# A price on changes of the matrix array's mode in a kernel's static order, with another order of its first loads

## The chip, the cores and the metric

The kernel runs on one core of one Trainium2 chip. The metric is the device time of one execution in microseconds (us); a lower one is better. Several runs are taken, and their median is given. A profile of one execution says what each engine did and when.

## What is computed

The reference runs a gated linear attention, a dense feed-forward layer and a layer of four experts, one after the other, all in float32.

```python
for t in range(S):                      # B, H, S, D = 2, 8, 768, 40
    m_new = np.maximum(f_gate[:, :, t] + m, i_gate[:, :, t])
    f_stab = np.exp(f_gate[:, :, t] + m - m_new)
    i_stab = np.exp(i_gate[:, :, t] - m_new)
    C = f_stab * C + i_stab * np.einsum('bhd,bhe->bhde', vt, kt)
    n = f_stab * n + i_stab * kt
    y[:, :, t] = o * (C @ qt) / np.maximum(np.abs(n @ qt), 1.0)
x = y as 1536 tokens x 320
h = x @ w_in                            # 320 x 2048
x = (h * (1.0 / (1.0 + np.exp(-1.702 * h)))) @ w_out
for e in range(4):                      # 320 x 1024, 1024 x 320
    out += p[:, e:e + 1] * (np.maximum(x @ w1[e], 0.0) @ w2[e])
```

## The kernel before, in words

**Attention.** The 768 steps are cut into 12 units of 64, and a unit holds both batches, 128 rows. A unit is worked in chunked form by `attn`: the decay of each pair of steps comes from two small matmuls with gate rows (`pe`, L343, and `pdc`, L347) and exponentials on ScalarE (`ex`, L353, and `dc`, L362); the scores `ps` (L380) are multiplied with `ex` to `pp` (L388); `pv` (L439, L442) is scores times values plus queries times the state; `sd` (L415) is what the unit adds to the state `st` (L424, L426), and `vw`, `ds` and `qs` (L397, L404, L368) scale values, state and queries, on VectorE or GpSimd. Then come the division and the output gate (L453 to L468), a transpose through TensorE (`pt`, L484), and its copy into the tiles `xb` in a high and a low half (L492, L496). `ps`, `sd` and `pv` run on 64 x 64 pieces of the array, two at a time; all other matmuls of the first 250 us use the whole 128 x 128 array. Most of the attention's PSUM tiles come from a pool of three (`at`).

**Dense layer.** The 2048 hidden features are 16 chunks. A chunk's weights come as 64-bit numbers (`raw`, L508, 704 KB) and are turned into a high and a low float32 half in seven operations by `conv` (L512 to L541) on ScalarE, VectorE and GpSimd. `layer1` (L574) and the second product (L663 to L668, called y here) run for three blocks of 512 tokens; the first block's chunks 0 to 3 are done in two halves of 256 tokens, since its later units are not there yet. Between the two products stand a tanh, a product, and a split into halves (`moe1`).

**Experts.** From about 262 us on all is in place and TensorE works through the four experts (L588, L592, L760 to L762).

**The order.** Nothing is scheduled at run time. Attention, conversion and dense layer are given to a planner, `Plan`, each piece with an engine, an estimated length, a due time (from the tables `DUE`, `T0`, `R256`, `R512`, `LOAD` and `RAW0`), what it depends on and which buffers it takes and gives. `Plan.order` walks through a modelled time: it takes the engine that can start first, and of that engine's pieces that can start then the one with the earliest due time. The code is emitted in that order, and the chip's engines then run their own instructions strictly in it. All loads are issued on SyncE's queue in planned order as well (`ring`), and eight of them may be under way. Strings such as `VW` or `GL` name the engine of each piece that VectorE (D) or GpSimd (P) can do. Until the first layer-1 step, gaps in TensorE's plan are filled with warm-up matmuls (`wps`, L791); later ones are left out.

Of the kernel before, what the change touches and what calls it, by code (L numbers as in the profile page):

```python
# [44 lines left out]
NR = 4  # L45
LANES = 8
XI = (0, 1, 3, 4, 2)
RAW0 = -39.51
LOAD = (-39.53, 5.33)
T0 = 7.75  # L50
R512 = 2.72
R256 = 3.14
DUE = (0.97, 2.56, -5.05, -4.98, 16.69, 15.23, 40.06, 43.14, 47.58, 64.09, 67.93, 31.23)
VW = "DPDPDDDDPPDD"
DS = "PDPPPDPDPDDP"
QS = "DPDDDDPPDPDP"
ADD = "DDPDPPPDDDDDPPDP"
LO = "PPPPDDDPPPDDDDDD"
HI = "AAAPAAAAAAAAPAAA"
GL = "PPQDDPPPQDQQPPDQDQPDDQPDQPPDPQQDQDPPQPDDPDDPDPQQPPDP"  # L60
# [3 lines left out]
class Plan:  # L64
# [9 lines left out]
    def add(self, eng, dur, due, fn=None, deps=(), take=(), give=(), lag=0.1, shared=False):  # L74
        self.ops.append((eng, dur, due, fn, {d for d in deps if d is not None}, take, give, lag, shared))
        return len(self.ops) - 1

    def order(self, slack):
        ops = self.ops
# [8 lines left out]
        port = 0.0  # L88
        while ready:
            cand = []  # L90
            for k, r in ready.items():
                eng, dur, due, _, _, take, _, _, shared = ops[k]
                if any(not self.tokens[t] for t in take):
                    continue
                t0 = max([r, free.get(eng, 0.0) if eng else 0.0] + [min(self.tokens[t]) for t in take])
                if shared:
                    t0 = max(t0, port)
                cand.append((t0, due, k))
# [3 lines left out]
            eng = ops[first[2]][0]  # L102
# [4 lines left out]
            eng, dur, _, _, _, take, give, lag, shared = ops[k]  # L107
# [5 lines left out]
            if shared:  # L113
                port = end
# [26 lines left out]
def body(tc, qk, kv, og, gates, gblk, wa, wb, dp, cst, out):  # L141
# [3 lines left out]
    with outer:  # L145
# [32 lines left out]
        PE, DV, AC, PO, SP = "PE", "DVE", "ACT", "POOL", "SP"  # L178
# [144 lines left out]
        def attn(u, due):  # L323
            ld = loads[u]
# [57 lines left out]
            m = P.add(PE, 1.2, due - 6, mm_s, deps=[ld["qk"]], take=[tok])  # L382
# [10 lines left out]
            if not last:  # L393
# [23 lines left out]
                sd = P.add(PE, 1.2, due - 3.6, mm_sd, deps=[vw, ld["kv"]], take=["at"], give=["vw"])  # L417
# [26 lines left out]
            pv = P.add(PE, 2.1 if u else 1.2, due - 4, mm_pv, deps=[pp, qs, ld["kv"], state.get(u)], take=["at"], give=["pp"] + (["qs"] if u else []))  # L444
# [59 lines left out]
        def conv(c, due):  # L504
# [38 lines left out]
            ld = ring(RAW0 + 2.5 * c if c < NR else due - 12, 2.25, load, take=["raw"] if c >= NR else [], deps=[] if c == 0 else [gate[4]] if c == 1 else gate[1][1] if c == 2 else reads)  # L543
# [395 lines left out]
```

## Time and profile before

| what | us |
|---|---|
| median of 3 runs (608.62 to 609.77) | 609.72 |
| profiled execution, its own time | 609.17 |
| span of the profile | 607.2 |
| TensorE busy, matmuls | 597.9 (98%) |
| VectorE busy | 254.6 (42%) |
| ScalarE busy | 185.1 (30%) |
| GpSimd busy | 153.9 (25%) |

The span is shorter than the execution's own time by 2.0 us, which lie around it. Busy shares are means over very different stages: attention and conversion are over by 160 us. PE is TensorE, ACT is ScalarE, DVE is VectorE, POOL is GpSimd and SP is SyncE. The starts of matmuls are recorded and their ends modelled, so the time that a group of them takes is best read from its start to the start of what follows. Some matmuls show as two passes, so 16 of the attention's appear as 32.

### The profile page before, as it was taken

The page shows a single profiled execution, that of the slowest core. Times are in us where ns is not written, and L with a number is a line of the kernel's source. Part 1 is how long each engine was busy: PE and PEld are TensorE (multiplying, and loading weights), DVE is VectorE, ACT ScalarE, POOL GpSimd, SP SyncE. Part 2 cuts the span into 40 slices and gives each one's busy share as a digit, 9 for nine tenths or more (in the row PEclk, how much of TensorE's full clock was granted, in tenths as well). Part 3 has the DMA queues.
Part 4 walks back from the last instruction along what each step waited for, and adds up shares of the span by engine and source line. Part 5 has one row for each costly group of instructions (what it writes and reads, how often), then busy time and mean ns, then how long its engine had stood idle before and what let it go on. Part 6 is the DMA issues. An engine that isn't in the chain of part 4 may idle for free.

```text
span 607.2 us, 10194 instructions
## 1 busy us (share of the span) xinstructions
PE 597.9 (98%) x4356; PEld 510.7 (84%) x4360; DVE 254.6 (42%) x457; ACT 185.1 (30%) x310; POOL 153.9 (25%) x126
## 2 busy tenths in 40 slices
PE   7999999999999999999999999999999999999997
PEld 3689888888888888889888888888888888888886
DVE  5699888887333422353231323232323131322313
ACT  4557466544333523341111111111111111111111
POOL 0473265521010331298504710006600000000000
PEclk8999999999999999999999999999999999999999
DMA  8876446610000010034301310002200000001101
GB/s 230 236 244 200 130 160 191 186 40 1 2 0 2 1 47 1 0 96 135 103 1 44 101 49 1 1 1 83 61 1 0 1 1 0 1 4 41 44 1 43
DMA packets 14432, 37.69 MB, mean 62 GB/s; under 512 B 2132, under 2 KB 4660, under 8 KB 14388
## 3 DMA queue, kind: packets, MB, share of 16 engines
q1 hardware_dynamic: 14066, 36.83, 20.1%
q8 instruction: 34, 0.56, 0.4%
q10 hardware_dynamic: 322, 0.21, 0.2%
q14 instruction: 10, 0.08, 0.1%
HBM read 34.75 MB, written 2.16 MB: 61 GB/s over the span
## 4 chain that ended last, share of the span: by engine, by line
PE 89%; DVE 4%; DMA 3%; ACT 1%; issue 1%; SPq 1%; POOL 0%; DVEq 0%; ACTq 0%
PE l L592 24%; PE l L574 16%; PE acc L762 9%; PE acc L761 9%; PE acc L760 9%; DMA raw<-in_wa_dram 3%; PE l L588 2%; PE yA L663 2%; PE yA L665 2%; PE yA L664 2%; PE yB L663 2%; PE yC L667 2%; PE yB L665 2%; PE yC L668 2%; PE yB L664 2%; PE pv L439 1%
## 5 line engine op out<-in xcount | busy, mean ns | idle before, releaser
L592 PE MATMUL l<-xb,w 128*128 128x512 f32 x616 | 146.2, 394 | 0.0
L592 PEld LDWEIGHTS l<-xb,w 128*128 128x128 f32 x616 | 113.9, 188 | 31.0 <-issue 8.0
L744 DVE SCALAR_TENSOR_TENSOR gl<-l,gh 128x512 fp32r<-128x512 f32 x88 | 60.9, 692 | 183.6 <-ACT gh L743 183.6
L743 ACT ACTIVATE gh<-l 128x512 fp32r<-128x512 f32 x88 | 52.7, 598 | 259.6 <-PE l L592 259.6
L762 PE MATMUL acc<-w,gl 128*128 128x320 f32 x384 | 118.7, 309 | 0.0
L761 PE MATMUL acc<-w,gh 128*128 128x320 f32 x384 | 118.6, 309 | 0.0
L760 PE MATMUL acc<-w,gh 128*128 128x320 f32 x384 | 118.5, 309 | 0.0
L574 PE MATMUL l<-xb,w 128*128 128x512 f32 (+1 forms) x480 | 111.8, 378 | 0.6 <-DVE xb L496 0.6
L574 PEld LDWEIGHTS l<-xb,w 128*128 128x128 f32 x480 | 85.7, 188 | 17.2 <-DVE xb L496 0.9
L760 PEld LDWEIGHTS acc<-w,gh 128*128 128x128 f32 x384 | 72.1, 188 | 1.1
L761 PEld LDWEIGHTS acc<-w,gh 128*128 128x128 f32 x384 | 72.1, 188 | 1.1
L762 PEld LDWEIGHTS acc<-w,gl 128*128 128x128 f32 x384 | 72.1, 188 | 0.0
L561 POOL TENSOR_TENSOR w<-rawf,w 128x704 fp32r<-128x704 f32 x32 | 55.4, 1732 | 2.7
L560 POOL TENSOR_SCALAR w<-rawf 128x704 fp32r<-128x704 f32 x32 | 24.9, 780 | 105.8 <-PE acc L762 96.8
L648 POOL TENSOR_TENSOR gl<-g,gh 128x512 fp32r<-128x512 f32 (+1 forms) x21 | 24.5, 1165 | 107.4 <-ACT gh L643 104.8
L631 ACT ACTIVATE g<-l 128x512 f32<-128x512 f32 (+1 forms) x52 | 29.3, 564 | 63.3 <-PE l L574 62.4
L635 DVE SCALAR_TENSOR_TENSOR g<-g,l 128x512 f32<-128x512 f32 (+1 forms) x38 | 24.1, 635 | 40.9 <-ACT g L631 40.7
L769 DVE SCALAR_TENSOR_TENSOR osb<-acc,pd,osb 128x320 f32<-128x320 f32 x36 | 17.3, 545 | 39.5 <-PE acc L762 39.5
L643 ACT ACTIVATE gh<-g 128x512 fp32r<-128x512 f32 (+1 forms) x38 | 22.5, 592 | 22.8 <-DVE g L635 22.8
L439 PE MATMUL pv<-kvt,pp 64*64 64x41 f32 x384 | 22.5, 228 | 0.0
L791 PE MATMUL wps<-wt 128*128 128x512 bf16 x73 | 20.4, 431 | 1.8 <-DVE wt L787 1.2
L439 PEld LDWEIGHTS pv<-kvt,pp 64*64 64x64 f32 x384 | 19.7, 133 | 2.4 <-issue 1.4
(113 smaller groups left out, 702.3 us busy)
## 6 DMA issues: line engine op xcount, KB each, us to landing
raw<-in_wa_dram SPq DMA_DIRECT2D x16, 704.0 KB
rawf<-in_wb_dram SPq DMA_DIRECT2D x32, 352.0 KB
qkt<-in_qk_dram SPq DMA_DIRECT2D x12, 416.0 KB
kvt<-in_kv_dram SPq DMA_DIRECT2D x12, 324.0 KB
ot<-in_og_dram SPq DMA_DIRECT2D x6, 320.0 KB
out_dram<-osb SPq DMA_DIRECT2D x12, 160.0 KB
const<-in_cst_dram SPq DMA_DIRECT2D x1, 228.0 KB
lsc<-hl SPq DMA_DIRECT2D x1, 192.0 KB
```

The lines of the kernel that those rows point to most:

```text
L439: te.matmul(out=half(pv, b)[:, h, :], lhsT=half(tiles["pp", u], b)[:, h, :], rhs=half(x, b)[:, h, D:KV], start=True, stop=u == 0)
L560: po.tensor_scalar(out=w[:, 0:WC], in0=raw, scalar1=1.0, scalar2=0.0, op0=ALU.mult, op1=ALU.add)
L561: po.tensor_tensor(out=w[:, WC:2 * WC], in0=raw, in1=w[:, 0:WC].bitcast(F32), op=ALU.subtract)
L574: te.matmul(out=ps[:, 0:n], lhsT=w[:, k0:k0 + 128], rhs=x[xi], start=(i == 0), stop=(i == 7))
L592: te.matmul(out=ps, lhsT=W[c][:, k0:k0 + 128], rhs=x[xi], start=False, stop=(i == 6))
L631: sc.activation(out=g[:, 0:nn], in_=tiles["l1", n][:, 0:nn], func=AF.Tanh, scale=0.851)
L648: eng.tensor_tensor(out=gl[:, 0:nn], in0=g[:, 0:nn], in1=gh[:, 0:nn].bitcast(F32), op=ALU.subtract)
L743: sc.activation(out=gh, in_=ps, func=AF.Relu)
L744: ve.scalar_tensor_tensor(out=gl, in0=ps, scalar=0.0, in1=gh.bitcast(F32), op0=ALU.max, op1=ALU.subtract)
L760: te.matmul(out=ps, lhsT=a, rhs=w[:, 384:WC], start=st, stop=False)
L761: te.matmul(out=ps, lhsT=a, rhs=w[:, WC + 384:2 * WC], start=False, stop=False)
L762: te.matmul(out=ps, lhsT=b, rhs=w[:, 384:WC], start=False, stop=sp)
```

## The change

Each piece of the planner's work gets a mark `half`, set for the scores, the state's sum and `pv`, which use 64 x 64 pieces of the array. Where TensorE's pieces compete, one that would change the mode has 8.59 us added to its due time, and 0.15 us to its length when taken. The second weight chunk's load (`c == 1`) now depends on the second unit's loads having been issued, where both hung on a copy of the gates (`gx`, L231) before. And the numbers of the tables and the strings are set anew. Nothing is computed otherwise. In line numbers, the new kernel is four lines longer from L128 on.

```diff
+MODE = 8.59
-RAW0 = -39.51
-LOAD = (-39.53, 5.33)
-T0 = 7.75
+RAW0 = -58.95
+LOAD = (-38.58, 16.7)
+T0 = 0.44
...
-DUE = (0.97, 2.56, -5.05, -4.98, 16.69, 15.23, 40.06, 43.14, 47.58, 64.09, 67.93, 31.23)
-VW = "DPDPDDDDPPDD"
+DUE = (0.16, 1.74, -5.43, -4.9, 16.37, 15.12, 32.37, 41.15, 48.48, 68.35, 78.86, 41.0)
+VW = "DPDPDPPDPPDP"
...
     def order(self, slack):
...
-        port = 0.0
+        port, mode = 0.0, False
...
-                cand.append((t0, due, k))
+                cand.append((t0, due + (MODE if eng == "PE" and half != mode else 0), k))
...
-            eng, dur, _, _, _, take, give, lag, shared = ops[k]
+            eng, dur, _, _, _, take, give, lag, shared, half = ops[k]
+            if eng == "PE":
+                dur += 0.15 if half != mode else 0
+                mode = half
...
-            m = P.add(PE, 1.2, due - 6, mm_s, deps=[ld["qk"]], take=[tok])
+            m = P.add(PE, 1.2, due - 6, mm_s, deps=[ld["qk"]], take=[tok], half=True)
...
-            ld = ring(RAW0 + 2.5 * c if c < NR else due - 12, 2.25, load, take=["raw"] if c >= NR else [], deps=[] if c == 0 else [gate[4]] if c == 1 else gate[1][1] if c == 2 else reads)
+            ld = ring(RAW0 + 2.5 * c if c < NR else due - 12, 2.25, load, take=["raw"] if c >= NR else [], deps=[] if c == 0 else [loads[1]["qk"] - 1, loads[1]["kv"] - 1] if c == 1 else gate[1][1] if c == 2 else reads)
```

The marks on `sd` and `pv` are set in the same way. Over the whole program the strings move these pieces from VectorE to GpSimd: one of 11 query scalings (L368), two of 11 value scalings (L397), one of 16 chunk additions (L528) and three of 52 low halves of the dense layer (L648); and one high half of a chunk from ScalarE to GpSimd (L533 for L535).

The first place is the load queue of SyncE at the start of the program (`raw_102` to `raw_104` are the first three weight chunks, `gs` and `gx` belong to the gates). Before:

```order
L284 DMA qkt<-in_qk_dram 104x1024
L508 DMA raw_102<-in_wa_dram 128x1408
L289 DMA kvt<-in_kv_dram 128x648
L181 DMA gx<-gs_99 96x1x128
L508 DMA raw_103<-in_wa_dram 128x1408
L284 DMA qkt<-in_qk_dram 104x1024
L289 DMA kvt<-in_kv_dram 128x648
L181 DMA lt<-hl 8x2x64 x2
L181 DMA rr<-hl 2x8x128
L181 DMA lsc<-hl 96x4x128
L303 DMA ot<-in_og_dram 128x640
L508 DMA raw_104<-in_wa_dram 128x1408
```

And now:

```order
L512 DMA raw_102<-in_wa_dram 128x1408
L288 DMA qkt<-in_qk_dram 104x1024
L293 DMA kvt<-in_kv_dram 128x648
L185 DMA gx<-gs_99 96x1x128
L288 DMA qkt<-in_qk_dram 104x1024
L293 DMA kvt<-in_kv_dram 128x648
L512 DMA raw_103<-in_wa_dram 128x1408
L185 DMA lt<-hl 8x2x64 x2
L185 DMA rr<-hl 2x8x128
L185 DMA lsc<-hl 96x4x128
L512 DMA raw_104<-in_wa_dram 128x1408
L307 DMA ot<-in_og_dram 128x640
```

The first chunk stands ahead of the first unit's queries, the second unit's loads ahead of the second chunk, and the third chunk ahead of the first output gates (`ot`).

The second place is TensorE at the first two layer-1 steps (`l`), where the third and fourth units come in. Before:

```order
L791 MATMUL wps<-wt 128x512
L574 MATMUL l_474<-xb_73,w 128x256 x8
L380 MATMUL ps<-qkt 64x64 x16
L343 MATMUL pe<-rr,lt 128x512 x2
L574 MATMUL l_517<-xb_73,w 128x256 x8
L347 MATMUL pdc<-rr,ltd 128x512 x2
L380 MATMUL ps<-qkt 64x64 x16
L415 MATMUL sd<-vw,kvt 64x41
L415 MATMUL sd<-vw,kvt 40x41
```

And now:

```order
L795 MATMUL wps<-wt 128x512
L578 MATMUL l_470<-xb_73,w 128x256 x8
L347 MATMUL pe<-rr,lt 128x512
L351 MATMUL pdc<-rr,ltd 128x512
L347 MATMUL pe<-rr,lt 128x512
L578 MATMUL l_491<-xb_73,w 128x256 x8
L351 MATMUL pdc<-rr,ltd 128x512
L384 MATMUL ps<-qkt 64x64 x32
L419 MATMUL sd<-vw,kvt 64x41
L419 MATMUL sd<-vw,kvt 40x41
```

The third unit's scores stood between the two steps and the fourth's behind; now both stand behind the second step, in one piece with `sd`, and the small decay matmuls are spread ahead of them.

The third place is ScalarE from the first unit's copy into `xb` to the third unit's exponential (`raw_104` and `raw_105` are the third and fourth chunk, `ot` the tanh of output gates). Before:

```order
L492 ACTIVATE xb_73<-pt 128x3x128
L535 ACTIVATE w<-cx 128x704
L516 ACTIVATE cr<-raw_104 128x704
L512 ACTIVATE cx<-raw_105 128x704
L516 ACTIVATE cr<-raw_105 128x704
L492 ACTIVATE xb_73<-pt 128x3x128
L309 ACTIVATE ot<-ot 128x640
L535 ACTIVATE w<-cx 128x704
L631 ACTIVATE g<-l_474 128x256
L353 ACTIVATE ex<-pe 128x512 x2
```

And now:

```order
L496 ACTIVATE xb_73<-pt 128x3x128
L539 ACTIVATE w<-cx 128x704
L496 ACTIVATE xb_73<-pt 128x3x128
L313 ACTIVATE ot<-ot 128x640
L516 ACTIVATE cx<-raw_105 128x704
L520 ACTIVATE cr<-raw_105 128x704
L357 ACTIVATE ex<-pe 128x512
L366 ACTIVATE dc<-pdc 104x512
L357 ACTIVATE ex<-pe 128x512
L366 ACTIVATE dc<-pdc 104x512
```

Both conversions of the fourth chunk now stand between the tanh and the exponentials `ex` and `dc`; before, they stood ahead of the second unit's copy.

## Rows read from the trace of the kernel before

**Rows 1.** Busy time by stage: us, then each engine's busy (instructions), PEclk, DMA share, GB/s.

```profile
30.00:130.00 100.00, 98.52 (x1400) 84.23 (x1399) 89.28 (x171) 61.48 (x104) 47.86 (x37) 1.00 0.57 175
...
160.00:600.00 440.00, 440.00 (x2343) 383.15 (x2342) 127.10 (x198) 96.80 (x162) 95.53 (x76) 1.00 0.10 28
```

**Rows 2.** TensorE in order of time, first 45 us: start, length, line, operands, idle before.

```profile
7.77 1.44 PE L380 MATMUL ps<-qkt 40*64 40x64 f32 x32 [2.13 <-DMA qkt<-in_qk_dram]
...
18.35 1.15 PE L380 MATMUL ps<-qkt 40*64 40x64 f32 x32
...
32.22 0.47 PE L574 MATMUL l<-xb,w 128*128 128x256 f32 x1
...
33.28 1.09 PE L574 MATMUL l<-xb,w 128*128 128x256 f32 x7 [0.60 <-DVE xb L496]
...
37.85 1.15 PE L380 MATMUL ps<-qkt 40*64 40x64 f32 x32 [0.28 <-DVE pp L388]
```

**Rows 3.** Waits of TensorE, whole span: us in total, times, longest.

```profile
PE pt L484 <- DVE yf L468: 0.5, 1, 0.5
```

**Rows 4.** TensorE in order of time, around three places of layer 1.

```profile
53.93 1.15 PE L380 MATMUL ps<-qkt 40*64 40x64 f32 x32
54.91 1.07 PE L415 MATMUL sd<-vw,kvt 64*64 64x41 f32 x32
...
80.50 0.39 PE L668 MATMUL yC<-gl,w 128*128 128x512 f32 x1
80.82 1.15 PE L380 MATMUL ps<-qkt 40*64 40x64 f32 x32
81.90 2.11 PE L574 MATMUL l<-xb,w 128*128 128x512 f32 x8
83.85 0.39 PE L663 MATMUL yA<-gh,w 128*128 128x512 f32 x1
...
130.92 3.79 PE L574 MATMUL l<-xb,w 128*128 128x512 f32 x16
134.54 0.39 PE L663 MATMUL yA<-gh,w 128*128 128x512 f32 x1
```

**Rows 5.** ScalarE in order of time, first 40 us.

```profile
9.29 0.83 ACT L512 ACTIVATE cx<-raw 128x704 f32<-128x704 f32 x1 [0.97 <-DMA raw<-in_wa_dram]
...
32.95 0.74 ACT L309 ACTIVATE ot<-ot 128x640 f32<-128x640 f32 x1 [1.01 <-DMA ot<-in_og_dram]
...
35.93 1.09 ACT L353 ACTIVATE ex<-pe 128x512 f32<-128x512 f32 x2 [1.13 <-PE pe L343]
```

**Rows 6.** VectorE in order of time, four places.

```profile
10.15 0.53 DVE L520 TENSOR_SCALAR cx<-cx 128x704 int32<-128x704 int32 x1 [2.93 <-ACT cx L512]
...
11.52 0.28 DVE L237 TENSOR_TENSOR gx<-gx 96x128 f32<-96x128 f32 x1
...
30.84 2.05 DVE L520 TENSOR_SCALAR cx<-cx 128x704 int32<-128x704 int32 x1 [0.18 <-ACT cx L512]
...
129.76 0.22 DVE L541 TENSOR_TENSOR w<-cx,w 128x64 fp32r<-128x64 f32 x1
```

**Rows 7.** Groups by line, VectorE then GpSimd: xcount, busy us, mean ns, idle before.

```profile
L368 DVE TENSOR_TENSOR qs<-dc,qkt 104x512 f32<-104x512 f32 x6 | 5.6, 941 | 0.1
...
L397 DVE TENSOR_TENSOR vw<-kvt,ex 128x328 f32<-128x328 f32 x7 | 3.5, 493 | 0.0
...
L528 DVE CUSTOM_DVE_ANT_0 cx<-cx,cr 128x1408 uint16<-128x1408 uint16 x9 | 9.3, 1035 | 0.0
...
L368 POOL TENSOR_TENSOR qs<-dc,qkt 104x512 f32<-104x512 f32 x5 | 7.4, 1474 | 11.5 <-ACT dc L362 11.5
...
L397 POOL TENSOR_TENSOR vw<-kvt,ex 128x328 f32<-128x328 f32 x4 | 3.2, 797 | 2.9 <-ACT ex L353 2.9
...
L533 POOL TENSOR_SCALAR w<-cx 128x704 fp32r<-128x704 f32 x2 | 3.8, 1892 | 0.1
```

**Rows 8.** GpSimd in order of time, one place.

```profile
30.83 1.68 POOL L528 TENSOR_TENSOR cx<-cx,cr 128x704 int32<-128x704 int32 x1 [2.13 <-ACT cx L512]
```

More of the change, by code (lines that the diff above doesn't have):

```diff
@@ L45 @@
 NR = 4
+MODE = 8.59
 LANES = 8
 XI = (0, 1, 3, 4, 2)
-RAW0 = -39.51
-LOAD = (-39.53, 5.33)
-T0 = 7.75
-R512 = 2.72
+RAW0 = -58.95
+LOAD = (-38.58, 16.7)
+T0 = 0.44
+R512 = 2.76
 R256 = 3.14
-DUE = (0.97, 2.56, -5.05, -4.98, 16.69, 15.23, 40.06, 43.14, 47.58, 64.09, 67.93, 31.23)
-VW = "DPDPDDDDPPDD"
[L55 to L60, printed above, removed]
+DUE = (0.16, 1.74, -5.43, -4.9, 16.37, 15.12, 32.37, 41.15, 48.48, 68.35, 78.86, 41.0)
+VW = "DPDPDPPDPPDP"
+DS = "DDPPDDDPPDPP"
+QS = "PPPPDDPPDDPD"
+ADD = "DDPPPDDPDPDPDDPP"
+LO = "PDPPPPDDDPDDDPDD"
+HI = "AAAAAAPAAPAAPAAA"
+GL = "PPPQPDPDDPQQDPDDQQPPPPDDQQPQPPPPPQQQPPQQPQDPQQPPDDPQ"
 GH = "A"
@@ L72, in __init__, with add @@
         self.tokens = {k: [0.0] * n for k, n in tokens.items()}
-    def add(self, eng, dur, due, fn=None, deps=(), take=(), give=(), lag=0.1, shared=False):
-        self.ops.append((eng, dur, due, fn, {d for d in deps if d is not None}, take, give, lag, shared))
+    def add(self, eng, dur, due, fn=None, deps=(), take=(), give=(), lag=0.1, shared=False, half=False):
+        self.ops.append((eng, dur, due, fn, {d for d in deps if d is not None}, take, give, lag, shared, half))
         return len(self.ops) - 1
@@ L91, in order @@
             for k, r in ready.items():
-                eng, dur, due, _, _, take, _, _, shared = ops[k]
+                eng, dur, due, _, _, take, _, _, shared, half = ops[k]
                 if any(not self.tokens[t] for t in take):
@@ L415, in mm_sd @@
                             te.matmul(out=half(sd, b, k)[:, h, :], lhsT=half(x, b)[:, h, 0:k], rhs=half(w, b)[:, h, :], start=True, stop=True)
-                sd = P.add(PE, 1.2, due - 3.6, mm_sd, deps=[vw, ld["kv"]], take=["at"], give=["vw"])
+                sd = P.add(PE, 1.2, due - 3.6, mm_sd, deps=[vw, ld["kv"]], take=["at"], give=["vw"], half=True)
                 def add_s():
@@ L442, in mm_pv @@
                             te.matmul(out=half(pv, b)[:, h, :], lhsT=half(tiles["qs", u], b, D)[:, h, :], rhs=half(tiles["st", u], b, D)[:, h, :], start=False, stop=True)
-            pv = P.add(PE, 2.1 if u else 1.2, due - 4, mm_pv, deps=[pp, qs, ld["kv"], state.get(u)], take=["at"], give=["pp"] + (["qs"] if u else []))
+            pv = P.add(PE, 2.1 if u else 1.2, due - 4, mm_pv, deps=[pp, qs, ld["kv"], state.get(u)], take=["at"], give=["pp"] + (["qs"] if u else []), half=True)
             P.add(None, 0, due, deps=[pv, state.get(u + 1)], give=["kv"], lag=0)
```

## The prediction

> **What bounds the kernel now.** I read the busy time by stage first, then TensorE's rows in order of time, then the rows of ScalarE, VectorE and GpSimd at the places that the order of the change touches. By stage [rows 1] TensorE is busy for 98.5 of the 100 us from 30 to 130 and for all of the 440 us from 160 to 600, at the full granted clock: the end is set by how much TensorE has to do and by when its first layer-1 step begins. VectorE is the next one: 89.3 of 100 us in the stage in which attention, weight conversion and layer 1 overlap, but 127 of 440 after it. So a gain must come from the first 160 us, and VectorE is the engine to distrust there; after 160 us both kernels run the same matmuls with everything ready.
>
> TensorE's rows [rows 2] show its losses at the start. It waits 2.13 us for the first queries, fills with warm-up matmuls, starts layer 1 at 32.22, and then waits in its first step: its other seven matmuls start at 33.28, 0.60 us of it named, so that the step lasts some 2.1 us. The fourth unit's scores begin at 37.85 after another 0.28. Behind these the list of waits names one more, 0.5 us [rows 3].
>
> **The price of a change of the array's mode.** The attention matmuls run on 64 x 64 pieces, everything else of this stage on 128 x 128. [Rows 4] let the price be taken apart at a lone score block between two full stretches. Full matmuls of 512 columns start 0.226 us apart (16 in 3.62 us, 130.92 to 134.54); the last before the scores takes 0.32 (80.50 to 80.82), 0.09 more. The 32 score passes take 1.08 us before a full matmul (80.82 to 81.90) and 0.98 where the mode stays (53.93 to 54.91), 0.10 more. The layer-1 step after them takes 1.95 (81.90 to 83.85) and not 1.81, 0.14 more. A round trip into the small mode and back so costs **0.33 us**, with no wait named.
>
> I counted the round trips in the two orders behind the first layer-1 step, without the row-split matmuls of layer 2, which are the same in both: **19 before, 8 now**. Eleven fewer are 3.6 us. The matmuls themselves are the same in number, except that 72 warm-up matmuls stand in place of 77. These cost only before layer 1 starts.
>
> **The start.** On the load queue the first weight chunk now goes ahead of the first queries, and the second unit's loads ahead of the second chunk. Before, the first scores got their queries at 7.77 [rows 2] and ScalarE its first chunk at 9.29 [rows 5]: 1.5 us apart. A chunk is 704 KB and the queries 416 KB; swapped, the chunk comes some 0.9 us sooner (416/704 of 1.5) and the queries at about 9.3. The chunk's conversion stands on VectorE ahead of the gate arithmetic: its first operation starts at 10.15, a second follows, and the gates at 11.52 without a wait named [rows 6]. Whether the gates' own data were there earlier the trace does not tell, so the gate chain gains between 0 and 0.9 us. I take 0.85, since VectorE waits for nothing else there. All that hangs on it (the decay rows, the third chunk, the output gates) moves with it. The later queries cost TensorE nothing: the second scores stand at 18.35, long after, and the wait falls on warm-up time. The second unit's earlier loads shorten nothing by themselves either, for the same reason: I price this part of the change at 0. Its cover is the warm-up stretch; without it the cost of the later second chunk would be its transfer, some 1.5 us, on ScalarE.
>
> What is late next is on ScalarE. Its order now has the gate tanh of the third unit (L309) and both conversions of the fourth chunk ahead of the third unit's exponentials. That tanh waited 1.01 us for its load and began at 32.95 [rows 5]. The same bytes are queued ahead of this load as before, so I let it come 0.85 us earlier, at 32.1. Then tanh 0.74, the two conversions at 0.83 each, and the exponential of 0.55 (half of the 1.09 for two): free at 35.1. TensorE meanwhile has two energy matmuls and a decay matmul in the three attention buffers of PSUM, and its next decay matmul needs one that this exponential frees. It gets there by about 33 (the first rival's start at 30.6, two steps of 1 us, three matmuls) and waits. At 35.1 it still has the decay matmul (0.23), the third unit's scores (0.98) and the entry (0.09) to do before it stands where the kernel before stood at 37.85: 36.4. So the start gives **1.4 us**, between bounds of 0 (the gate chain gains nothing, so the exponentials come no sooner; for a loss they would have to come later than today, with the same bytes ahead of them) and 2.7 (the first rival). One round trip lies inside this wait; ten are left, **3.3 us**.
>
> **What takes something back.** Ahead of the last chunk's first layer-1 step TensorE has 3.3 us less of mode changes and, by the order, one unit's product with the values less (64 passes, about 1.9 us by the 0.98 for 32): 5.2 us. The chunk is ready just in time today: its last VectorE operation starts at 129.76 and takes 0.22 [rows 6], the step begins at 130.92 [rows 4], 0.94 us of slack. By the order VectorE gives GpSimd one query scaling, two value scalings and one chunk addition, 0.94 + 2 x 0.49 + 1.04 = 3.0 us [rows 7], and is left with 86.3 of its 89.3. At its share of today (0.893) that takes 96.7 us, where TensorE leaves 94.8. Less the slack, the last chunk is **0.9 us late**. Below this is 0 (VectorE's idle tenth is filled); above, the next two cases.
>
> The sum against the profiled execution, 609.17 us: 609.17 - 1.4 - 3.3 + 0.9 = **605.4 us**. The median of the runs shown stands 0.55 above that execution, which I leave in the range. What a measurement can tell from no change is about 0.2%, 1.2 us.
>
> **A rule that speaks against the change.** While GpSimd's chunk addition ran (30.83, 1.68 us, [rows 8]) VectorE's operation on another chunk took 2.05 us, where the same operation had taken 0.53 at 10.15 [rows 6]: one of the two stands while the other runs. The change gives GpSimd 1.47 + 2 x 0.80 + 1.68 + 1.89 = 6.6 us more of work [rows 7, 8] ahead of the last chunk (one query scaling, two value scalings, one addition, one high half). By the sum above VectorE is lighter by 3.0; if every added GpSimd operation stood in its way, it would be heavier by 3.6, with the result of the fourth case. The Trainium skill (SBUF, section Who interferes with whom) says that such a pair of ports goes to whoever issues first for the whole instruction, and the other "fully blocks". By that rule the sum lies nearer the fourth case than by my count; the row at 30.84 agrees with it. How often the two meet in the new order no row of before can show; today GpSimd is busy for 47.9 of the 100 us and VectorE still does its work in 89.3 [rows 1].
>
> **The rivals.**
> 1. *Nothing late at the start.* If the tanh's load comes in time, TensorE is bound by its own filling: five warm-up matmuls fewer (1.1 us), 0.5 less of waiting for queries (ten more warm-up matmuls of 0.2 us ahead of the first scores take it from 5.64 to 7.7, the queries come at 9.3: 1.6 and not 2.1) and no wait of 1.1 in the first step: 2.7, with all eleven round trips: 609.17 - 2.7 - 3.6 = 602.9. For it: the load queue is issued a little sooner at every place. Against: the tanh already waited today.
> 2. *VectorE takes it all.* The work it hands over comes back as standing still for GpSimd, and it needs the 100 us of today. TensorE's 5.2 us are then waits but for the slack: 609.17 - 4.7 + 4.3 = 608.8, no change. For it: 89 of 100 us busy, and chunks ready just in time. Against: part of its idle tenth is waiting for TensorE itself.
> 3. *The price is not paid per change.* The 0.14 us after a small block may belong to the weight load of the first full matmul and stay, and grouped blocks may wait for their multiplications: then only the start's 1.4 less 0.9 is gained, 608.7. The order shows that the changes are really gone, and 0.09 and 0.10 stand at each end, so little is left for this case.
> 4. *Slower: GpSimd shuts VectorE out.* 86.3 + 6.6 = 92.9 us of work at today's share take 104.0; 104.0 - 94.8 - 0.94 = 8.3 late: 609.17 - 4.7 + 8.3 = 612.8. It decides from some 4.7 us of lateness on, that is when half of the added GpSimd work meets VectorE.
>
> **How the numbers follow.** My forecast (604 to 607.5) has 0.62, the first rival 0.13, the second 0.11, the third 0.05, the fourth 0.09. Faster by over 0.2% is the forecast and the first: 0.75, with a little of the second at its lower edge, 0.76. Within 0.2%: 0.15. Slower: 0.09. The range runs from 602.0 (the first rival and half a run's scatter) to 609.6 (past the second and third); the fourth is left out, with the tails.
>
> **What would show it.** Right: a lone step after scores still at 1.95 us, but eight such places; the first step near 30.5 with no wait inside it; a wait of about 2 us on TensorE before a decay matmul near 33 to 35, named by an exponential; VectorE busy above 0.9 from 30 to 125; the last chunk's step near 121 to 123, and from there on TensorE some 4 us ahead. Wrong: waits of TensorE for VectorE's multiplications or for a chunk that add up to 4 us or more, or the first step still at 32 or later.

## The result: 1.5% slower, against a forecast of 0.7% faster

| what | us |
|---|---|
| changed kernel, median of 4 runs (613.57 to 620.54) | 619.58 |
| before, median of 4 runs beside it (608.62 to 609.77) | 609.62 |
| ratio, with its 95% interval | 1.0148 [1.0117, 1.0179] |
| profiled execution of the changed kernel, its own time and its span | 619.24 and 617.3 |

The forecast was 605.4 us, the range 602.0 to 609.6, the chance of slower 0.09. The time lies outside the range and on the other side. None of the four rivals describes it. One of the four executions, 613.57 us, ran at a mean granted clock of 0.994; the other three, at 0.978 to 0.983, took 619.24 to 620.54.

The busy tenths of the profile's page show the place in one line, TensorE's granted clock in 40 slices of 15.4 us:

```profile
PEclk9967998999999999999999999999999999999999
```

By windows of ten us (time, then busy time of each engine with its instructions, granted clock, DMA share), as in [rows 1] for the kernel before:

```profile
core 0: us, PE busy (x) PEld busy (x) DVE busy (x) ACT busy (x) POOL busy (x), PEclk, DMA share, GB/s
30.00:40.00 10.00, 7.44 (x84) 6.31 (x84) 4.62 (x10) 6.28 (x13) 4.15 (x5) 0.84 0.78 274
40.00:50.00 10.00, 10.00 (x196) 10.00 (x194) 3.94 (x13) 2.18 (x4) 6.57 (x8) 0.50 0.43 120
50.00:60.00 10.00, 10.00 (x109) 9.60 (x108) 6.89 (x16) 6.62 (x14) 3.17 (x3) 0.81 0.44 142
...
90.00:100.00 10.00, 8.76 (x62) 7.33 (x59) 7.55 (x17) 2.85 (x5) 5.69 (x5) 0.66 0.65 215
```

Before, the clock was 1.00 from 30 to 130 us [rows 1]. Now it is 0.50 for all of 40 to 50 us, the lower of its two levels, 1.2 instead of 2.4 GHz. TensorE is busy for 10.00 of these 10 us, so a busy share alone hides the loss. It is 1.00 from 60 to 90 and from 100 to 130 us. The shortfall of the four disturbed windows is 1.6 + 5.0 + 1.9 + 3.4 = 11.9 us of full clock.

TensorE's waits from the first layer-1 step on, in total, times, longest one:

```profile
PE pdc L351 <- ACT ex L357: 2.6, 1, 2.6
PE ps L384 <- DVE st L428: 1.2, 1, 1.2
PE sd L419 <- issue: 1.0, 1, 1.0
PE yA L669 <- DVE gl L652: 0.8, 1, 0.8
PE sd L419 <- DVE vw L401: 0.3, 1, 0.3
```

And TensorE's rows around the first of them:

```profile
30.89 1.30 PE L578 MATMUL l<-xb,w 128*128 128x256 f32 x8
...
32.72 1.11 PE L578 MATMUL l<-xb,w 128*128 128x256 f32 x8
36.39 0.50 PE L351 MATMUL pdc<-rr,ltd 128*128 128x512 f32 x1 [2.56 <-ACT ex L357]
36.87 3.68 PE L384 MATMUL ps<-qkt 40*64 40x64 f32 x64
...
58.62 2.08 PE L384 MATMUL ps<-qkt 40*64 40x64 f32 x64
```

The first layer-1 step starts 1.3 us sooner than before [rows 2], and the wait predicted for this place is there and bears the predicted name. The scores begin at 36.87, but that is not yet the place where TensorE stood at 37.85 before [rows 2]: there the third unit's 32 score passes were done, as TensorE's row of before shows, and here they are the first half of the 64:

```profile
34.31 1.15 PE L380 MATMUL ps<-qkt 40*64 40x64 f32 x32
```

At full clock they take 0.98 us, and TensorE would stand at that place at 37.85, exactly as before. And the clock falls right behind the wait, while TensorE works through the long block of small pieces that the price has put together: the 64 passes that take 2.08 us at 58.62 take 3.68 here. ScalarE's rows show the wait's origin:

```profile
33.67 0.74 ACT L313 ACTIVATE ot<-ot 128x640 f32<-128x640 f32 x1 [3.41 <-DMA ot<-in_og_dram]
34.31 0.81 ACT L516 ACTIVATE cx<-raw 128x704 f32<-128x704 f32 x1
35.03 0.82 ACT L520 ACTIVATE cr<-raw 128x704 int32<-128x704 uint32 x1
35.76 0.58 ACT L357 ACTIVATE ex<-pe 128x512 f32<-128x512 f32 x1
```

**The balance.** So the start gives nothing, and all of the difference of the spans, 617.3 - 607.2 = 10.1 us, comes from the fourth unit's scores on. Ten round trips less give 3.3 back. The waits from there on are 1.2 + 1.0 + 0.8 + 0.3 = 3.3, where before there was one of 0.5 [rows 3]. So 10.1 + 3.3 - 2.8 = 10.6 us are left for the clock, and 11.9 are what its windows lack. In this execution it accounts for the sign and for nearly all of the size. It is not the whole of the loss: the execution of 613.57 us, at a mean clock of 0.994, is still 4.0 us above the kernel before.

### The profile page after: what moved, and what is told of

Same layout as the page of the kernel before. It is cut to its first block, busy times and chain, and to the rows that moved or that the text cites. A ratio compares the mean times of both kernels' runs of the same rounds, so it can differ in the third digit from the quotient of the medians.

```text
span 617.3 us, 10184 instructions
## 1 busy us (share of the span) xinstructions
PE 604.1 (98%) x4351; PEld 519.6 (84%) x4355; DVE 249.1 (40%) x450; ACT 183.7 (30%) x309; POOL 156.3 (25%) x134
## 4 chain that ended last, share of the span: by engine, by line
PE 91%; DMA 3%; ACT 2%; DVE 2%; issue 1%; SPq 0%; DVEq 0%; ACTq 0%
PE l L596 23%; PE l L578 16%; PE acc L766 9%; PE acc L765 9%; PE acc L764 9%; PE l L592 2%; PE yA L667 2%; PE pv L443 2%; PE ps L384 2%; PE yA L669 2%; PE yB L667 2%; PE yB L669 2%; PE yA L668 2%; PE yB L668 2%; PE yC L671 2%; PE yC L672 2%
## 5 line engine op out<-in xcount | busy, mean ns | idle before, releaser
L652 POOL TENSOR_TENSOR gl<-g,gh 128x512 fp32r<-128x512 f32 (+1 forms) x24 | 28.0, 1171 | 86.4 <-ACT gh L647 72.8
L639 DVE SCALAR_TENSOR_TENSOR g<-g,l 128x512 f32<-128x512 f32 (+1 forms) x35 | 22.1, 632 | 39.6 <-ACT g L635 39.4
L647 ACT ACTIVATE gh<-g 128x512 fp32r<-128x512 f32 (+1 forms) x35 | 20.5, 588 | 17.6 <-DVE g L639 17.6
L443 PE MATMUL pv<-kvt,pp 64*64 64x41 f32 x384 | 25.6, 241 | 0.1
L443 PEld LDWEIGHTS pv<-kvt,pp 64*64 64x64 f32 x384 | 22.2, 147 | 2.6 <-issue 1.1
L446 PE MATMUL pv<-st,qs 40*64 40x41 f32 x352 | 24.3, 241 | 0.0
```

The source lines that it names most:

```text
L443: te.matmul(out=half(pv, b)[:, h, :], lhsT=half(tiles["pp", u], b)[:, h, :], rhs=half(x, b)[:, h, D:KV], start=True, stop=u == 0)
L652: eng.tensor_tensor(out=gl[:, 0:nn], in0=g[:, 0:nn], in1=gh[:, 0:nn].bitcast(F32), op=ALU.subtract)
```

## Experiments: the early wait

Medians of the kernel before, run beside the experiments, were 609.1 in this group. The first theory was that TensorE's wait lets its clock fall.

**Fill the wait.** Twelve warm-up matmuls ahead of the fourth unit's decay matmul, all else as changed.

```diff
+            if k in self.ahead:
+                self.ahead[k]()
...
+            P.ahead = {dec[3]: lambda: [keep_warm() for _ in range(12)]}
```

> The changed kernel with twelve warm-up matmuls put on TensorE ahead of the fourth unit's decay matmul, where TensorE waited 2.6 us for the third unit's exponential; nothing else is moved, and the wait for the exponential stays. Theory (that wait lets TensorE's clock fall, and it stays at half through the small-piece matmuls that follow): no half clock between 37 and 54 us, 7.4 us less than the changed kernel, 611 to 613 us. Rival 1 (small-piece matmuls in a long block lower the clock by themselves): the clock falls all the same, 617 to 621 us. Rival 2 (the clock is a bystander and the waits cost the time): as the changed kernel, 617 to 621 us, with the clock at full.

Measured: 613.8 us (9 runs, ratio 1.0076 [1.0045, 1.0107]), just above the theory's range. TensorE's row:

```profile
35.15 2.76 PE L797 MATMUL wps<-wt 128*128 128x512 bf16 x12
```

And the windows:

```profile
30.00:40.00 10.00, 10.00 (x112) 6.98 (x111) 5.63 (x14) 6.54 (x13) 4.63 (x4) 1.00 0.89 305
40.00:50.00 10.00, 8.17 (x213) 8.08 (x209) 8.42 (x19) 3.98 (x7) 6.94 (x9) 0.91 0.45 120
```

The matmuls that take the wait's place compute nothing that is used, and the kernel gains 5.8 us by the medians: the long block behind them now runs at full clock. What follows it is a new wait of 1.8 us. Of the nine executions one, 620.22 us at a mean clock of 0.981, is like the changed kernel; the others, at 0.991 or more, take 611.96 to 614.15. Filling the wait so makes the early fall rare. What is left, 4.7 us above the kernel before, has other parts: in the profiled execution waits of 4.5 us behind these scores, and shorter falls of the clock.

**Take the wait away.** The third unit's gate tanh moves behind the fourth unit's exponentials on ScalarE.

```diff
-        for k, _, _ in self.order(slack):
+        seq = [k for k, _, _ in self.order(slack)]
+        for k, after in self.move:
+            seq.remove(k)
+            seq.insert(seq.index(after) + 1, k)
+        for k in seq:
...
+            P.move = [(sig[2], exd[3])]
```

> The changed kernel with one ScalarE instruction moved: the gate tanh of the third and fourth unit goes behind the two pairs of exponentials that it stood ahead of. Theory (in-order wait on ScalarE makes TensorE wait, and the wait makes the clock fall): the 2.6 us and the half clock both go, 608 to 611 us. Rival 1 (the long block of small pieces lowers the clock): 2.6 us less, about 616 to 617 us. Rival 2 (VectorE bounds the stage anyway): 616 us or more, with new waits of TensorE for VectorE.

Measured: 614.6 us (6 runs, 1.0086 [1.0058, 1.0114]), so neither as low as expected nor unchanged. The wait ahead of the block is gone, but one has come up inside it, as TensorE's row shows:

```profile
40.85 0.34 PE L450 MATMUL pv<-st,qs 40*64 40x41 f32 x3 [1.28 <-issue]
```

And the clock falls there, in the window's row:

```profile
40.00:50.00 10.00, 9.15 (x124) 9.07 (x124) 6.83 (x17) 1.59 (x4) 4.39 (x6) 0.53 0.52 156
```

**Longer wait.** The changed kernel with the price set to 3 in place of 8.59; the order is the same up to 66 us.

> The changed kernel with a price of 3 and not 8.59: the same order up to 66 us, the same wait for the exponential, 13 round trips and not 8. Theory (the wait at 33 to 36 us and the clock after it cost the most): the half clock from 37 to 54 us is there as in the changed kernel; 1.7 us more for five round trips, less what the two later waits cost (up to 5 us with the second fall of the clock): 615 to 621 us. Rival (the strong grouping of small pieces is the cause): 609 to 613 us.

Measured: 621.82 us (4 runs, 1.0202 [1.0162, 1.0241]), just above the expected range. The profiled execution waited 4.4 us at the same place, with the clock at 0.50 from 40 to 50 us and at 0.65 in the ten us after. All four executions have a mean clock of 0.977 to 0.981.

**The price alone.** The tables and loads of before, with only the marks and the price of the change.

```diff
+MODE = 8.59
...
+                cand.append((t0, due + (MODE if eng == "PE" and half != mode else 0), k))
...
+            m = P.add(PE, 1.2, due - 6, mm_s, deps=[ld["qk"]], take=[tok], half=True)
```

> The kernel before with the price on a change of mode alone; tables, strings and loads as before. TensorE makes 10 round trips behind the first layer-1 step, not 19 (the changed kernel makes 8). Theory: 9 x 0.33 = 3.0 us are gained, 606 to 608 us, unless the new order has a wait of 2 us or more ahead of small pieces; then the clock falls and it is 612 us or more. Rival (the price itself is the fault, since grouped small pieces wait for VectorE and GpSimd): slower than before by 2 us or more with the clock at full.

Measured: 618.25 us (4 runs, 617.49 to 632.31, 1.0143 [1.0108, 1.0178]). The rival is right: its clock is 1.00 from 30 to 80 us, and it is slow for another reason. Its first layer-1 step begins at 36.31 us, not at 32.22 [rows 2], and three of its waits are:

```profile
PE sd L419 <- DVE st L428: 1.6, 1, 1.6
PE yA L669 <- DVE gl L652: 1.4, 1, 1.4
PE yA L667 <- ACT gh L647: 1.4, 1, 1.4
```

With the tables of before the price makes an order in which TensorE waits for VectorE and ScalarE. With the new tables only 3.3 us of such waits are named, beside the early one. (Its clock from 80 to 110 us is between 0.83 and 0.91, around those waits.)

## Experiments: what lowers the clock, measured alone

Is it the wait, or the long row of small pieces? Both stand together in the changed kernel. So I took the kernel before and its eleventh unit's scores, near 142 us, where TensorE waits for nothing. The scores are computed twelve times there, eleven of them in vain. Before took 609.4 us in this group.

```diff
+                for i in range(12 if u == 10 else 1):
                     for h in range(H):
                         for b in range(B):
```

> The kernel before, with the scores of the eleventh unit (near 142 us, where TensorE waits for nothing) computed twelve times in a row instead of once, 11 x 0.98 = 10.8 us more of 64 x 64 pieces and nothing else. Theory (TensorE's clock falls in a long uninterrupted stretch of small pieces by itself, as it did in the run with the tanh moved): the granted clock falls to 0.5 inside the stretch some 4 to 8 us after its start, its later scores take about 1.9 us instead of 0.98, and the time is 622 to 628 us. Rival (small pieces do no harm, only the wait ahead of them does): granted clock 1.00 all along, every score block 0.98 us, 609.5 + 10.8 = 620.3 us.

Measured: 619.55 us (617.43 to 622.75, 1.0158 [1.0097, 1.0219]). The rival is right. The twelve blocks in TensorE's rows:

```profile
145.87 11.41 PE L381 MATMUL ps<-qkt 40*64 40x64 f32 x384
```

The window over them:

```profile
146.00:157.00 11.00, 11.00 (x380) 11.00 (x381) 1.03 (x2) 1.49 (x3) 0.13 (x1) 1.00 0.02 4
```

Small pieces for 11.4 us on end leave the clock at 1.00. (The profiled execution is the one of 622.75 us; its clock was low elsewhere, 0.75 from 30 to 40 us.) Now with a wait ahead of them:

```diff
+                if u == 10:
+                    te.matmul(out=ps.rearrange("p h t -> p (h t)"), lhsT=lt[:, u, :], rhs=lt[:, 0:4, :].rearrange("p u t -> p (u t)"), start=True, stop=True)
+                    for _ in range(4):
+                        sc.activation(out=ps, in_=ps, func=AF.Copy)
```

> As the run before it, with a wait put ahead of the twelve score blocks: one full-array matmul into their tile and four copies of that tile in place on ScalarE (some 0.6 us each), for which TensorE waits about 2.5 us. At full clock this is 609.5 + 10.8 + 0.3 + 2.5 = 623.1 us. Theory of the wait (a wait of that length and small pieces behind it lower the clock at once, as at 36.8 us in the changed kernel): half clock within 1 us of the stretch's start and nearly to its end, 628 to 635 us, and the fall comes earlier than in the run without the wait by about the length of the wait or more. Rival (only the length of the small stretch counts): the fall comes as late after the stretch's start as without the wait, or not at all, 623 to 630 us.

Measured: 633.0 us, three of four executions between 632.4 and 634.4 and the fourth at 621.9. The profiled one (632.4), its row and its windows:

```profile
146.26 18.90 PE L385 MATMUL ps<-qkt 40*64 40x64 f32 x384 [2.51 <-ACT ps L381]
```

```profile
146.00:157.00 11.00, 10.74 (x236) 10.74 (x238) 0.50 (x1) 1.70 (x4) 0.00 (x0) 0.61 0.01 3
157.00:165.00 8.00, 8.00 (x154) 7.97 (x150) 0.00 (x0) 0.00 (x0) 0.00 (x0) 0.50 0.01 2
```

The same 384 passes take 18.90 us and not 11.41. The fall comes some 2.5 us into the stretch, not within one as I had written, and it does not come in every execution. And the same wait with 48 full-array matmuls behind it, in place of eleven of the blocks:

> The same ScalarE wait, with 48 full-array matmuls of 512 columns (48 x 0.227 = 10.9 us, overwritten by the scores) behind it in place of eleven of the twelve score blocks; the scores are then computed once. At full clock 623.3 us. Theory (the wait alone does little, the small pieces behind it keep the clock low): full clock or one short stretch of 3.4 us at half, 622.5 to 625.5 us. Rival (the wait alone lowers the clock, whatever follows): half clock for 10 us or more, 628 us or more.

Measured: 624.57 us (623.21 to 625.98, 1.0258 [1.0236, 1.028]), as expected. Row and window:

```profile
144.86 12.77 PE L383 MATMUL ps<-lt 128*128 128x512 f32 x48 [2.51 <-ACT ps L381]
```

```profile
146.00:157.00 11.00, 11.00 (x43) 8.94 (x43) 0.00 (x0) 0.29 (x1) 0.00 (x0) 0.87 0.00 0
```

The clock falls here too, but soon returns: 12.7 us for what takes 10.9. So it takes both, where the fall comes: a wait ahead of it, and small pieces that keep the clock down, where 48 full matmuls brought it back. The wait with full matmuls behind it cost at most 2.7 us beyond its length (the highest of four runs, 626.0, against 623.3 at full clock), the small pieces alone nothing, both together 9.9 (633.0 against 623.1).

Two more asked whether a few full matmuls in between help: four of 512 columns behind every third block, without the wait and with it.

```diff
+                    if i and i % 3 == 0:
+                        for _ in range(4):
+                            te.matmul(out=ps.rearrange("p h t -> p (h t)"), lhsT=lt[:, u, :], rhs=lt[:, 0:4, :].rearrange("p u t -> p (u t)"), start=True, stop=True)
```

> As the run with twelve score blocks, with four full-array matmuls of 512 columns (into the same tile, overwritten by the next scores) behind every third block: 3 x (4 x 0.226 + 0.33) = 3.7 us more, at full clock 624.0 us. Theory (full matmuls in between keep the clock up): granted clock 1.00 through the stretch, 623.5 to 624.5 us. Rival (the total of small pieces counts, whatever lies between): half clock in the stretch as in the run without them, above 626 us.

> The twelve score blocks behind the ScalarE wait, as in the run that took 633.0 us, now with four full-array matmuls behind every third block (3.7 us more). At full clock all of it would be about 626.9 us. Theory (it takes a stall and small pieces behind it to lower the clock, and full matmuls bring it back): half clock, if at all, only up to the first or second of the full matmuls, 626.5 to 630 us. Rival (once low, the clock stays low until the whole mixed stretch is over): 634 to 638 us.

Measured: 623.38 us without the wait (clock 1.00 in the stretch; since the plain stretch keeps it too, this tells nothing apart), and with it 626.7, 630.6, 639.2 and 639.2 us in four executions. The profiled one is the first, with the clock at 1.00 through the whole stretch behind the same wait of 2.51 us. The two at 639.2, with a mean clock of 0.973 over the whole execution, lost 12 us, more than the stretch without full matmuls did. No trace shows these two; by their times groups of four don't bring the clock back, and my theory falls on this point.

## Experiments: the order of the first loads

I had priced the swap at the gate chain's gain of 0.85 us. The kernel before with nothing but the swapped loads:

```diff
+            P.move = [(loads[0]["qk"] - 1, w_ld[0]), (loads[1]["kv"] - 1, gate[4] - 1), (loads[1]["qk"] - 1, gate[4] - 1)]
```

> The kernel before with only the load queue's order of the changed kernel at the start: the first weight chunk ahead of the first queries, the second unit's queries and values ahead of the second chunk; all else as before. My prediction's step (the gate chain moves 0.85 us forward with the first chunk): the gates' first operation on VectorE near 10.7 instead of 11.52, the first layer-1 step near 31.4, 608.3 to 609.3 us. Theory after the changed kernel's trace (the gates' copy stands behind one more load's worth of bytes and lands later): the gates' first operation waits for that copy and starts at 11.8 or later, the first layer-1 step no earlier than 32.2, 609.3 to 610.5 us.

Measured: 611.33 us (10 runs, 610.3 to 612.14; ratio 1.0018 [0.9991, 1.0044] against a scattered group of before), above what either expected; the interval leaves room for no loss at all. VectorE's and TensorE's rows:

```profile
9.23 0.53 DVE L526 TENSOR_SCALAR cx<-cx 128x704 int32<-128x704 int32 x1 [2.52 <-ACT cx L518]
...
12.71 0.29 DVE L241 TENSOR_TENSOR gx<-gx 96x128 f32<-96x128 f32 x1 [2.03 <-DMA gx<-gs]
...
36.42 1.30 PE L581 MATMUL l<-xb,w 128*128 128x256 f32 x8
```

The first chunk is converted earlier, as predicted (9.23 instead of 10.15), but the gates' first operation comes at 12.71 instead of 11.52 [rows 6]. It waits for its own copy. SyncE's rows of the copy, before and in the changed kernel, whose first loads have the same order (6.55 us in this run):

```profile
7.06 0.74 SPq L181 DMA_DIRECT2D gx<-gs  x1
```

```profile
6.62 0.74 SPq L185 DMA_DIRECT2D gx<-gs  x1
```

The copy is issued sooner, behind the same three loads in another order, and lands later; the second unit's queries and values now follow right behind it. Which of the two delays it no run tells. That the swap delays it several traces do: in all six with the swapped loads (11.87 to 13.35) the operation waits 0.99 to 2.03 us for the copy; in the six that share the start of the kernel before (10.93 to 11.67) it never does.

The first layer-1 step starts at 36.42 and not at 32.22 [rows 2] (32.10 to 33.60 in those six traces). Of these 4.2 us only about two reach the end; the 1.4 us of waits in and behind the first step [rows 2, 3] are gone. In the changed kernel's profile the gates' row reads:

```profile
11.87 0.29 DVE L241 TENSOR_TENSOR gx<-gx 96x128 f32<-96x128 f32 x1 [0.99 <-DMA gx<-gs]
```

Now the other way round, the changed kernel with the loads of before:

```diff
+            P.move = [(w_ld[0], loads[0]["qk"] - 1), (w_ld[1], gate[4] - 1)]
```

> The changed kernel with only its first loads put back into the order of the kernel before (first queries ahead of the first chunk, second chunk ahead of the second unit's loads); its table and its price stay. Theory (the main loss is the wait for the third unit's exponential and the clock that falls with the small pieces behind it; the loads' order adds one or two us): the wait stays near 2 us, the clock falls near 37 us again, 614 to 618.5 us. Rival (the loads' order is the cause of the loss): no fall of the clock near 37 us, 611 us or less.

Measured: 613.61 us (8 runs, 1.0073 [1.0043, 1.0104]): 6.0 us better than the changed kernel by the medians, 4.9 when each is taken against its own runs of before, and below the theory's range, though above the rival's. One of the eight, 618.31 us at a mean clock of 0.983, is like the changed kernel. In the profiled execution the gates came even later (13.85) and the first step at 34.26, but the gate tanh began only 0.87 us behind that step, where the changed kernel had 33.67 - 30.89 = 2.78:

```profile
34.26 1.30 PE L585 MATMUL l<-xb,w 128*128 128x256 f32 x8
...
37.88 0.50 PE L355 MATMUL pdc<-rr,ltd 128*128 128x512 f32 x1 [0.68 <-ACT ex L361]
```

```profile
35.13 0.74 ACT L317 ACTIVATE ot<-ot 128x640 f32<-128x640 f32 x1 [1.50 <-DMA ot<-in_og_dram]
```

```profile
30.00:40.00 10.00, 9.11 (x112) 6.73 (x111) 7.13 (x19) 6.53 (x13) 5.05 (x5) 1.00 0.93 321
40.00:50.00 10.00, 8.71 (x229) 8.45 (x226) 8.38 (x21) 5.07 (x9) 8.28 (x10) 1.00 0.47 126
```

A wait of 0.68 us ahead of the same long block, and the clock stays at 1.00. By these two traces an earlier start with a longer wait behind it was worth less than a later start with a short one.

## Experiments: is the gain there at all?

If waits and the clock are all that is wrong, removing the named waits should show the 3.6 us of the mode changes. The first mix takes the changed kernel with the tanh moved, puts the chunk additions of chunks 3, 7 and 11 on VectorE, and moves two pieces of VectorE's order; the second also has the loads of before.

```diff
+                eng = ve if c in (3, 7, 11) else eng
...
+            P.move = [(sig[2], exd[3]), (w_op[7], state[7]), (state[8], state[8] - 1)]
```

> The changed kernel with TensorE's named stalls of the first 110 us taken out one by one: the third unit's gate tanh behind the fourth unit's exponentials on ScalarE, three chunk additions (chunks 3, 7, 11) on VectorE instead of GpSimd, so that the fourth unit's query scaling ends sooner, the last weight operation of chunk 7 behind the state's sum on VectorE, and one other state's sum ahead of a division. Theory (the loss is stalls, and the clock that falls where a stall meets small pieces): against the run with only the tanh moved (614.6) the stall of 1.3 us in the values' products goes, and with it the 10.2 us of half clock (5.1 us), a stall of 1.2 us near 88 and 1.7 us of half clock there, 1.0 and 1.7 near 108: 603 to 607 us. Rival (the long blocks of small pieces that the price makes lower the clock without a stall): half clock again near 40 us, 611 us or more.

> As the run before it, with the first loads in the order of the kernel before (first queries ahead of the first chunk, the second chunk ahead of the second unit's loads). Theory (the swap made the gates' copy and the queries later): the first queries come 2 us sooner, the gates' first operation near 11.5 instead of 11.9 to 12.9, and the time is 0.5 to 1.5 us below the run before it. Rival (the swap is neutral, its cover is the warm-up stretch): within 0.4 us of it.

Measured: 612.84 us (1.007 [1.0045, 1.0095]) and 609.0 us (10 runs, 0.9989 [0.9971, 1.0007]). In the first a wait of 1.39 us inside the small pieces was still there, and the clock was 0.64 from 40 to 50 us, with a time in the rival's range. In the second the wait was 0.3 us and the clock 1.00. The loads are worth 3.8 us there, not the 0.5 to 1.5 expected; by the two traces that wait hangs on them.

Two more mixes removed what the profiles named next: chunk 7's last operation behind the gate product and chunk 3's low half on VectorE; then a conversion behind the half that TensorE waited for, and the fifth unit's product ahead of the sixth's (with one low half, `gl_op[3]`, moved along).

```diff
+            P.move = [(sig[2], exd[3]), (w_op[7], my_op[6]), (w_op[3], state[4]), (ca_op[10], gr_op[11]), (pp_op[5], pp_op[4]), (gl_op[3], pp_op[4]), (state[8], state[8] - 1), (w_ld[0], loads[0]["qk"] - 1), (w_ld[1], gate[4] - 1)]
```

> The mixed version that took 609.0 us with two of its remaining stalls removed: the last weight operation of chunk 7 behind the product with the output gate (TensorE waited 1.3 us for that product near 83 us, and the clock fell for 3.4 us behind it), and the low half of chunk 3 on VectorE instead of GpSimd, behind the fourth unit's state (GpSimd's operation had made VectorE's gate product near 41 us last 2.16 us instead of 0.49, and TensorE waited 0.9 us). Theory (named stalls and the clock that falls with them are all that separates it from the sum of the gains): 609.0 - 1.3 - 1.7 - 1.0 = 605.0, between 603.5 and 606.5 us, faster than the kernel before. Rival (each stall removed shows up elsewhere, VectorE being full): 608 to 610 us.

> The second mixed version (609.25 us) with the two stalls taken out that its profile names: the first conversion of the eleventh chunk on ScalarE behind the high half that TensorE waited 1.8 us for near 91 us (that conversion waits for a buffer that GpSimd frees at 93 us), and the fifth unit's scores multiplied ahead of the sixth's on VectorE (0.5 us near 54 us, in small pieces, with 3.4 us of half clock behind it). Theory (named stalls and their clock are what is left): 609.25 - 1.8 - 0.5 - 1 = 606, between 604.5 and 607.5 us, faster than the kernel before. Rival (stalls only move on, the order is as good as the engines beside TensorE allow): 608 to 610 us.

Measured: 609.25 us (12 runs, 1.001 [0.9986, 1.0035]) and 609.18 us (12 runs, 1.0009 [0.9994, 1.0024]), both level with before. The rival is right both times: the removed waits went, and others took their place. The last one's profile is of its lowest execution, 607.02 us with a span of 604.9, at a clock of 1.00 in every window from 30 us on. Its waits from 30 us on:

```profile
PE yA L678 <- DVE gl L661: 2.0, 1, 2.0
PE sd L425 <- ACT ot L317: 0.3, 1, 0.3
PE pt L494 <- DVE yf L478: 0.2, 1, 0.2
```

Its balance agrees with the price of the mode. The span is 607.2 - 604.9 = 2.3 us less. Its scores begin at 35.64, so with the 0.98 us of the third unit's passes it stands at 36.62 where before stood at 37.85: 1.2 of these. The waits from there on are 2.5 and not 0.5 [rows 3]. So 2.3 - 1.2 + 2.0 = 3.1 us are gained elsewhere, where ten round trips are 3.3. This is a remainder of two single executions, not a measurement of the price. No version that I ran is measurably faster than the kernel before.

## Why the prediction was wrong, point by point

**The clock, which no step had.** I read the granted clock of 1.00 off [rows 1] and carried it into the new order. My own forecast contained a wait of two us on TensorE and, right behind it, the longest block of small pieces in the program, and I priced the wait as its length. This step failed: it cost its length and up to 8.5 us more (1.6 + 5.0 + 1.9 of the windows). The Trainium skill (TensorE: Matmul & The Clock Gate, section HAM oscillation — how this bites in real kernels) says that a wait between bursts of matmuls can make the chip lower the clock again. It was a rule that spoke against this change, and the rivals lacked it. The traces agree for the most part: in three kernels with waits of 2.5 to 4.4 us ahead of small pieces the clock fell to half, with the wait filled the block behind it ran at 1.00; but one trace with a wait of 2.51 us ahead of small pieces (full matmuls behind every third block) shows no fall.

**The start: right mechanism, wrong chain.** The first step at 30.89, the tanh and the two conversions ahead of the exponential, and the wait on it of about two us (2.56) came as predicted. But the 36.4 that I forecast is the place behind the third unit's scores, and TensorE would have stood there at 37.85 even at full clock (36.87 + 0.98): the start gives 0.0 us and not 1.4, the lower of my bounds. The step that failed is "the gate chain gains between 0 and 0.9 us. I take 0.85". Only the conversion came earlier; the gates then waited 0.99 us for their copy and began 0.35 later than before, at 11.87. I had noted that the trace does not tell whether the gates' data were there, and took the favourable end. I had also ruled out a loss "with the same bytes ahead of them": the loads ahead of the gates' copy are indeed the same three, and it landed later all the same. The tanh of the third unit began at 33.67, 0.7 later than before [rows 5] and 1.6 later than the 32.1 that I let it come at. One execution says little here, however: five other traces with the start of the kernel before have this tanh at 34.07 to 35.25, and with the loads put back the gates came at 10.92 to 11.26 in three traces and at 13.85 in a fourth.

**"I price this part of the change at 0."** The second unit's loads ahead of the second chunk belong to a swap that makes the kernel before two us slower by the medians, within the scatter; in the changed kernel it is 5 to 6 of its 10 us. By the two traces it sets how far the first step runs ahead of the tanh's load, and so the wait. The cover I named, the warm-up stretch, hides the loads from TensorE, but VectorE's gate chain came later. Which of the two swapped loads does it was not tried.

**The price of the mode: nothing against it.** TensorE's rows show 19 round trips before and 8 now, as counted, and the balance of the last mix leaves 3.1 us for ten of them, where I had 3.3. The price was not measured by itself.

**VectorE's lateness: too small.** I had 0.9 us at the last chunk. It came in other places instead, 2.8 us more of waits than before, none at that chunk; 2.3 of the 3.3 are named for VectorE, and for the 1.0 ahead of a state's sum the profile names nothing. Two are of the kind of the fourth rival. VectorE's and GpSimd's rows near 82 and 88 us:

```profile
81.66 2.59 DVE L652 TENSOR_TENSOR gl<-g,gh 128x512 fp32r<-128x512 f32 x1 [0.30 <-ACT gh L647]
...
88.57 1.89 DVE L544 TENSOR_TENSOR w<-cx,w 128x640 fp32r<-128x640 f32 x1
...
106.37 0.69 DVE L652 TENSOR_TENSOR gl<-g,gh 128x512 fp32r<-128x512 f32 x1
```

```profile
80.74 1.30 POOL L372 TENSOR_TENSOR qs<-dc,qkt 104x512 f32<-104x512 f32 x1
82.00 1.70 POOL L532 TENSOR_TENSOR cx<-cx,cr 128x704 int32<-128x704 int32 x1
...
88.22 1.55 POOL L372 TENSOR_TENSOR qs<-dc,qkt 104x512 f32<-104x512 f32 x1 [0.89 <-ACT dc L366]
```

The same form takes 0.69 us at 106.37, where GpSimd is idle, and 2.59 through a query scaling and a chunk addition, and TensorE waits 0.8 for it. Near 88 us a weight operation takes 1.89 beside a query scaling (0.82 at 79.21), and the state that TensorE waits 1.2 us for comes behind it. The Trainium skill (SBUF — State Buffer, section Who interferes with whom) says that a VectorE operation with two inputs in SBUF contends with GpSimd's reads from there. The trace agrees. It bears on two waits of 0.8 and 1.2 us here, not on the 8.3 of that rival.

Put together with what the runs showed: 609.17 - 0.0 - 3.3 + 2.8 + 10.6 = 619.3, where 619.24 was measured. That the sum closes is no proof of each term: the 10.6 came from this balance, and only the windows' 11.9 stand beside it independently.

**What stays open.** Why the clock falls in some executions of one kernel and not in others (613.57 beside 619.24 to 620.54; 621.9 beside 633.0; 626.7 beside 639.2), why the gates' copy lands later, and how much of the loss near 90 us is the wait for the state and how much the clock behind it: I did not separate the two there.

## What to carry to other kernels

A wait on TensorE is not priced by its length alone: look at what stands behind it. Where a long block of 64 x 64 pieces followed here, the granted clock could halve and stay there, so read the clock of each window after a change, above all where TensorE is busy for 10 of 10 us. And grouping work of one kind by a price removes a small cost per change and takes away the slack in which other engines prepared the next piece; in the mixes here the two came out about equal.

## What the runs showed that I had not expected

The clock stayed at 1.00 through 11.4 us of nothing but 64 x 64 pieces, and fell to 0.50 in the same pieces behind a wait of 2.51 us, for 18.90 us instead of 11.41. Four full matmuls (some 1.1 us) between them did not bring it back in two of four executions, by their times. And the start of layer 1 moved by more than the whole change was worth, with little effect by itself: 30.89 in the changed kernel, 32.22 before, 34.26 and 36.42 with the loads' order exchanged, while the slowest of the four times belongs to the earliest start.
